# One FFN pass per batch with weights loaded by expert, fp16 loads, and k/v pooling on TensorE

## Chip, cores and metric

The kernel runs on one core of a Trainium2 chip. The metric is device time in microseconds; three runs of the kernel before gave 723.87, 724.64 and 724.81 us (median 724.64).

## What is computed

Attention with pooled keys and values, then a mixture of experts that sends each token to one of eight FFNs. q, k and v are 8 batches x 8 heads x 576 tokens x 64; tokens number 4608, the model dimension is 512, the hidden one 1024.

```python
def _attn_ref(q, k, v):
    k_p = k.reshape(B, H, Sp, 8, D).mean(axis=3)
    v_p = v.reshape(B, H, Sp, 8, D).mean(axis=3)
    scores = scale * np.matmul(q, k_p.transpose(0, 1, 3, 2))
    attn = softmax(scores)
    return np.matmul(attn, v_p)

def _moe_ref(x, expert_emb, tau, w1, w2):
    xn, en = x / norm(x), expert_emb / norm(expert_emb)
    logits = xn @ en.T / tau
    expert_idx = np.argmax(logits, axis=1)
    gate_w = softmax(logits)[np.arange(N), expert_idx]
    for e in range(E):
        mask = expert_idx == e
        h = np.maximum(x[mask] @ w1[e], 0.0)
        out[mask] = gate_w[mask, None] * (h @ w2[e])
```

The norm, the softmax and the calls that join the two parts are shortened here. All inputs and the output are fp32 in HBM. On the inputs that the reference draws, all 576 tokens of a batch choose the same expert (7, 5, 5, 1, 7, 4, 3, 4 for the eight batches); a chunk of 128 tokens that lies across two batches can hold two.

## The kernel before

Five compute engines work from their own queues: PE (TensorE, with its weight loads shown as PEld), DVE (VectorE), ACT (ScalarE), POOL (GpSimd) and SP, which here only issues DMAs. A scheduler orders the work of each engine.

*Weights.* `w1_sb` and `w2_sb` hold all eight experts in bf16. POOL issues 16 DMAs (lines 78 and 82) that read fp32 and write bf16; from the ninth on each waits until the eighth before it has landed.

*Attention*, a static loop over 8 batches and 8 heads. SP loads `q_in`, `k_in` and `v_in` of one head as 72 partitions x 512 fp32 (lines 195 to 197), with two buffers each. DVE sums eight keys and eight values (lines 201, 205). PE transposes the pooled keys twice and the pooled values once (210 to 214) and q in four fp32 pieces (220), and DVE copies q to bf16 (226). Per head two matmuls of 288 columns make the scores (238, on the two halves of the rows), and ACT the exponential (247). For every piece of at most 128 tokens PE makes eight matmuls of 73 columns (255): 64 outputs, the sum, and eight products with the expert embedding. DVE divides (262, 264), ACT squares (269), and four transposes (286) put x into `xt_all`.

*Routing* (lines 296 to 416) runs once on all 36 chunks: the expert that is most frequent in each chunk, and a list of up to twelve further (chunk, expert) pairs.

*FFN* (`ffn`, lines 112 to 142). 36 chunks of 128 tokens with their first expert, then always 12 spare passes, for pairs of the list or for nothing. A pass has 8 matmuls of 512 columns into `h_ps` (120), a relu with the gate as scale on ACT (127), 8 transposes (132), a DVE copy (135), and 8 matmuls of 512 columns into `y_ps` (137). The expert is a register value, so the address of the weights in each of the 16 matmuls is worked out at run time. A spare pass reads the output rows back, adds and stores them (lines 457 to 459).

Of the kernel before, what the change touches and what calls it, by code (L numbers as in the profile page):

```python
# [22 lines left out]
@with_exitstack
def kernel(
# [28 lines left out]
    const_pool = ctx.enter_context(tc.tile_pool(name="const", bufs=1))  # L53
    wpool = ctx.enter_context(tc.tile_pool(name="wpool", bufs=1))
    route_sb = ctx.enter_context(tc.tile_pool(name="route_sb", bufs=1))

    ident_bf = const_pool.tile([128, 128], BF16)
    make_identity(nc, ident_bf)
    ident_f16 = const_pool.tile([128, 128], FP16)
    make_identity(nc, ident_f16)  # L60
    ident_f32 = const_pool.tile([128, 128], FP32)
    make_identity(nc, ident_f32)
    tri_cand = const_pool.tile([NCAND, NCAND], BF16)
    make_upper_triangular(nc, tri_cand, val=1.0, diag=False)
    ones_col = const_pool.tile([128, 1], BF16)
    nc.vector.memset(ones_col, 1.0)
    iota8 = const_pool.tile([128, 8], FP32)
    nc.gpsimd.iota(iota8, pattern=[[1, 8]], base=0, channel_multiplier=0,
                   allow_small_or_imprecise_dtypes=True)
    cgrid = const_pool.tile([1, NCAND], FP32)  # L70
    nc.gpsimd.iota(cgrid, pattern=[[1, NCHUNK], [0, MAXE - 1]], base=0,
                   channel_multiplier=0, allow_small_or_imprecise_dtypes=True)
    enT_sb = const_pool.tile([64, H, E], FP16)

    w1_sb = wpool.tile([128, E, 4, F], BF16)
    w2_sb = wpool.tile([128, E, 8, DM], BF16)
# [12 lines left out]
    ssq_all = route_sb.tile([128, NCHUNK], FP32)

    gateoh_all = route_sb.tile([128, NCHUNK, E + 1], BF16)
    rank_e_f = route_sb.tile([1, NCHUNK, MAXE], FP32)
    rank_v_f = route_sb.tile([1, NCHUNK, MAXE], FP32)
    rank_e0_i = route_sb.tile([1, NCHUNK], I32)
    extras_i = route_sb.tile([1, NEXTRA, 3], I32)

    def seg_list(b):
        segs = []
        t0 = b * S
        t = t0  # L100
        while t < t0 + S:
            c = t // 128
            seg_end = min((c + 1) * 128, t0 + S)
            segs.append((t - t0, seg_end - t, c, t - c * 128))
            t = seg_end
        return segs

    with tc.tile_pool(name="ps_m1", bufs=2, space=bass.MemoryType.PSUM) as ps_m1:

        def m1():  # L110
            return ps_m1.tile([128, 512], FP32, name="m1")

        moe_pools = {}

        def ffn(xt_tile, gm, e_val):
            h_ps = moe_pools['h'].tile([128, F], FP32, name="h_ps")
            y_ps = moe_pools['y'].tile([128, DM], FP32, name="y_ps")
            for w in range(4):
                for fb in range(2):
                    nc.tensor.matmul(  # L120
                        out=h_ps[:, ts(fb, 512)],
                        lhsT=xt_tile[:, w, :],
                        rhs=w1_sb[:, ds(e_val, 1), w, ts(fb, 512)].squeeze(1),
                        start=(w == 0), stop=(w == 3),
                    )
            h_sb = moe_pools['sb'].tile([128, F], BF16, name="h_sb")
            nc.scalar.activation(out=h_sb, in_=h_ps, func=AF.Relu, scale=gm)  # L127
            ht_ps0 = m1()
            ht_ps = ht_ps0.bitcast(BF16)[:, 0:1024].rearrange("p (w t) -> p w t", t=128)
            h_sb8 = h_sb.rearrange("p (d w) -> p w d", w=8)  # L130
            for w in range(8):
                nc.tensor.transpose(out=ht_ps[:, w, :], in_=h_sb8[:, w, :],  # L132
                                    identity=ident_bf)
            ht_sb = moe_pools['sb'].tile([128, 8, 128], BF16, name="ht_sb")
            nc.vector.tensor_copy(out=ht_sb, in_=ht_ps)  # L135
            for w in range(8):
                nc.tensor.matmul(  # L137
                    out=y_ps,
                    lhsT=ht_sb[:, w, :],
                    rhs=w2_sb[:, ds(e_val, 1), w, :].squeeze(1),  # L140
                    start=(w == 0), stop=(w == 7),
                )
            return y_ps

        with tc.tile_pool(name="init_sb", bufs=1) as init_sb:
            emb_sb = init_sb.tile([E, DM], FP32)
            nc.sync.dma_start(out=emb_sb, in_=moe_expert_emb)
            emb_sq = init_sb.tile([E, DM], FP32)
            emb_ssq = init_sb.tile([E, 1], FP32)
            nc.scalar.activation(out=emb_sq, in_=emb_sb, func=AF.Square,  # L150
                                 accum_out=emb_ssq)
            emb_nrm = init_sb.tile([E, 1], FP32)
            nc.scalar.activation(out=emb_nrm, in_=emb_ssq, func=AF.Sqrt)
            nc.vector.tensor_scalar_add(out=emb_nrm, in0=emb_nrm, scalar1=1e-6)
            emb_rcp = init_sb.tile([E, 1], FP32)
            nc.vector.reciprocal(out=emb_rcp, in_=emb_nrm)
            nc.scalar.mul(out=emb_rcp, in_=emb_rcp, mul=1.0 / tau)
            enp_sb = init_sb.tile([E, DM], FP32)
            nc.vector.tensor_scalar_mul(out=enp_sb, in0=emb_sb, scalar1=emb_rcp)
            ent_ps = m1()  # L160
            ent_v = ent_ps[0:64, 0:H * E].rearrange("p (h e) -> p h e", e=E)
            for h in range(H):
                nc.tensor.transpose(out=ent_v[:, h, :], in_=enp_sb[:, ts(h, 64)],
                                    identity=ident_f32[:E, :E])
            nc.scalar.copy(out=enT_sb, in_=ent_v)

# [328 lines left out]
```

## Time and profile before

| | |
|---|---|
| median of three runs | 724.64 us |
| span of the profiled execution | 722.3 us (its own time is not given apart from the runs) |
| PE / PEld busy | 451.4 us (62%) / 206.7 us (29%) |
| DVE busy | 305.5 us (42%) |
| ACT busy | 157.5 us (22%) |
| POOL busy | 11.2 us (2%) |
| moved by DMA | 61.41 MB |

Busy shares are averages over stages that differ, so the stages have to be looked at one by one. A matmul's busy time is modelled and pipelined with its neighbours; the distance between the starts of two instructions says more. "issue" means that an engine waited for nothing that the profile shows: its own instruction stream held it.

### The profile page before, as it was taken

How to read it: one execution, taken by the hardware profiler on the slowest of the kernel's cores; microseconds unless marked ns; L12 is line 12 of the kernel's file. 1: busy time of each engine (PE TensorE's matmuls, PEld its weight loads, DVE VectorE, ACT ScalarE, POOL GpSimd, SP SyncE). 2: the span in 40 equal slices, each digit the busy share in tenths (PEclk: the TensorE clock that was granted, in tenths of full speed). 3: DMA queues.
4: the chain of work that ended last, by engine and by line, in shares of the span. 5: the costliest groups of instructions: out<-in, count | busy, mean ns of one | idle time of the engine just before them, and what ended most of it. 6: DMA issues, size and time to landing. Idle time of an engine off the chain costs nothing.

```text
span 722.3 us, 8926 instructions
## 1 busy us (share of the span) xinstructions
PE 451.4 (62%) x2261; PEld 206.7 (29%) x2284; DVE 305.5 (42%) x668; ACT 157.5 (22%) x263; POOL 11.2 (2%) x30
## 2 busy tenths in 40 slices
PE   0010035646465565655388888888888888888774
PEld 0000023434344343443132323222222222223221
DVE  0112169788778777843844522212212212122221
ACT  2000023343333334344311111111111111111110
POOL 4000000000000000000000000000000000000000
PEclk9999999999999999999999999999999999999996
DMA  7999954325243423400000101010011001111112
GB/s 160 229 230 229 209 160 123 113 93 156 74 131 93 128 94 106 131 21 30 0 30 30 45 30 44 30 45 30 30 45 44 30 30 45 44 59 60 59 73 88
DMA packets 27130, 61.41 MB, mean 85 GB/s; under 512 B 3528, under 2 KB 3528, under 8 KB 25040
## 3 DMA queue, kind: packets, MB, share of 16 engines
q1 hardware_dynamic: 24784, 44.07, 18.8%
q0 software_dynamic: 2304, 16.78, 11.2%
q8 instruction: 27, 0.44, 0.3%
q14 instruction: 15, 0.12, 0.1%
HBM read 65.03 MB, written 12.58 MB: 107 GB/s over the span
## 4 chain that ended last, share of the span: by engine, by line
PE 47%; DVE 23%; DMA 15%; issue 10%; ACT 4%; DVEq 0%; ACTq 0%; another core or an unknown queue 0%; SPq 0%
PE y_ps L137 18%; PE h_ps L120 17%; DMA k_in<-in_k_dram 12%; DVE vpx_all L205 6%; DVE kp_sb L201 5%; DVE x_sb L264 4%; PE m L220 3%; PE m L132 3%; PE xps L255 3%; DVE qT_sb L226 2%; ACT xps L269 2%; PE s_ps L238 2%; ACT at_tok L247 1%; DVE rsum L262 1%; DMA o_sb<-out_dram 1%
## 5 line engine op out<-in xcount | busy, mean ns | idle before, releaser
L137 PE MATMUL y_ps<-w_sb,ht_sb 128*128 x372 | 141.0, 387 | 31.8 <-issue 7.7
L120 PE MATMUL h_ps<-w_sb,xt_all 128*128 x278 | 102.1, 384 | 29.7 <-PE h_ps L120 8.0
L127 ACT ACTIVATE h_sb<-h_ps,gm 128x1024 bf16<-128x1024 f32 x48 | 53.5, 1114 | 290.0 <-PE h_ps L120 274.2
L437 DVE COPY y_sb<-y_ps 128x512 f32<-128x512 f32 x36 | 24.9, 692 | 129.6 <-PE y_ps L137 129.6
L137 PEld LDWEIGHTS <-ht_sb 128*128 128x128 bf16 x384 | 36.9, 97 | 134.3 <-issue 119.0
L201 DVE TENSOR_REDUCE kp_sb<-k_in 72x64 bf16<-72x512 f32 x64 | 64.7, 1010 | 19.5 <-DMA k_in<-in_k_dram 19.2
L205 DVE TENSOR_REDUCE vpx_all<-v_in 72x64 f16<-72x512 f32 x64 | 64.3, 1008 | 19.7 <-DMA v_in<-in_v_dram 19.6
L135 DVE COPY ht_sb<-m 128x1024 bf16<-128x1024 bf16 x48 | 32.9, 686 | 86.2 <-PE m L132 73.7
L220 PE MATMUL m<-ident_f,q_in 72*128 72x72 f32 x256 | 45.6, 338 | 27.9 <-DMA q_in<-in_q_dram 27.9
L247 ACT ACTIVATE at_tok<-s_ps 72x576 f16<-72x576 f32 x64 | 41.4, 647 | 76.0 <-PE s_ps L238 76.0
L226 DVE CAST qT_sb<-m 128x288 bf16<-128x288 f32 x64 | 29.1, 455 | 65.0 <-PE m L220 64.8
L120 PEld LDWEIGHTS <-xt_all 128*128 128x128 bf16 x288 | 27.0, 97 | 82.9 <-issue 79.3
L255 PE MATMUL xps<-vpx_all,at_tok 72*128 72x73 f16 (+1 forms) x320 | 36.8, 253 | 14.2 <-DVE dtmp L273 11.1
L286 PE MATMUL m<-ident_bf,x_sb 128*128 128x128 bf16 (+1 forms) x160 | 22.8, 293 | 36.4 <-DVE x_sb L264 36.4
L214 PE MATMUL kvt_ps<-ident_f,vpx_all 72*64 72x72 f16 x64 | 17.2, 269 | 45.2 <-DVE vpx_all L205 44.7
L238 PE MATMUL s_ps<-qT_sb,kpT_sb 64*72 64x288 bf16 x128 | 29.1, 428 | 23.8 <-ACT at_tok L247 16.0
L220 PEld LDWEIGHTS m<-ident_f,q_in 72*128 72x128 f32 x256 | 33.9, 219 | 33.7 <-issue 29.7
L120 PE MATMUL h_ps<-w_sb,xt_in 128*128 x95 | 34.5, 377 | 8.6 <-PE h_ps L120 5.1
L269 ACT ACTIVATE xps<-x_sb 128x512 f32<-128x512 bf16 (+1 forms) x40 | 24.0, 601 | 63.0 <-DVE x_sb L264 62.9
L210 PE MATMUL kvt_ps<-ident_bf,kp_sb 72*64 72x72 bf16 x64 | 16.3, 255 | 34.1 <-DVE kp_sb L201 32.5
L132 PEld LDWEIGHTS <-h_sb 128*128 128x128 bf16 x384 | 31.5, 146 | 20.7 <-issue 15.6
L255 PEld LDWEIGHTS <-at_tok 72*128 72x128 f16 (+1 forms) x320 | 26.6, 134 | 28.1 <-issue 20.5
(101 smaller groups left out, 294.8 us busy)
## 6 DMA issues: line engine op xcount, KB each, us to landing
w_sb<-in_moe_w_dram POOLq DMA_DIRECT2D x16, 1024.0 KB, 43.6
q_in<-in_q_dram SPq DMA_DIRECT2D x64, 144.0 KB
k_in<-in_k_dram SPq DMA_DIRECT2D x64, 144.0 KB
v_in<-in_v_dram SPq DMA_DIRECT2D x64, 144.0 KB
out_dram<-y_sb SPq DMA_DIRECT2D x36, 256.0 KB
o_sb<-out_dram SPq DMA_DIRECT2D x12, 256.0 KB
out_dram<-o_sb SPq DMA_DIRECT2D x12, 256.0 KB
emb_sb<-in_moe_expert_emb_dram SPq DMA_DIRECT2D x1, 16.0 KB
```

Of the source, the lines that this page charges most:

```text
L120: nc.tensor.matmul(out=h_ps[:, ts(fb, 512)], lhsT=xt_tile[:, w, :], rhs=w1_sb[:, ds(e_val, 1), w, ts(fb, 512)].squeeze(1), start=(w == 0), ...
L127: nc.scalar.activation(out=h_sb, in_=h_ps, func=AF.Relu, scale=gm)
L132: nc.tensor.transpose(out=ht_ps[:, w, :], in_=h_sb8[:, w, :], identity=ident_bf)
L137: nc.tensor.matmul(out=y_ps, lhsT=ht_sb[:, w, :], rhs=w2_sb[:, ds(e_val, 1), w, :].squeeze(1), start=(w == 0), stop=(w == 7),)
L201: nc.vector.tensor_reduce(out=kp_sb, in_=k_in.rearrange("g (j d) -> g d j", j=POOL), axis=AX.X, op=ALU.add)
L205: nc.vector.tensor_reduce(out=vpx_all[:, h, 0:64], in_=v_in.rearrange("g (j d) -> g d j", j=POOL), axis=AX.X, op=ALU.add)
L220: nc.tensor.transpose(out=qt_m[:, ts(sblk, G)].bitcast(FP32)[:, 0:G], in_=q_in[:, ts(sblk, 128)], identity=ident_f32[:G, :G])
L226: nc.vector.tensor_copy(out=qT_sb, in_=qt_m[:, 0:4 * G])
L238: nc.tensor.matmul(out=s_ps[:, j, 0:STP], lhsT=kpT_sb[ts(j, 64), h], rhs=qT_sbs[h][ts(j, 64)], start=True, stop=True,)
L247: nc.scalar.activation(out=at_tok, in_=s_tok, func=AF.Exp, scale=escale)
L255: nc.tensor.matmul(out=xps[psl, h, 0:73], lhsT=at_tok_tiles[h][:, loc0:loc0 + L], rhs=vpx_all[:, h, :], start=True, stop=True,)
L269: nc.scalar.activation(out=xps[psl, :, 0:64], in_=x_sb[psl], func=AF.Square, accum_out=ssq_all[psl, cidx:cidx + 1])
```

## The change

Nearly the whole body is new.

- All loads go through POOL's queue and write fp16. q, k and v of a batch come in three DMAs (`load_qkv`): partitions are 2 heads x 64 groups of 9 tokens, with 4 head pairs beside each other. `load_w` loads one expert's `w1` and `w2` by a register value, into one of three fixed buffers; PE addresses only fixed buffers.
- Pooling of k and v is 18 matmuls of 512 columns per batch with a 0/1 matrix `pmat`, which POOL builds with four selects after the loads of batches 0 and 1.
- q is transposed as fp16. The products with the expert embedding become 20 matmuls per batch on the transposed x, in `_route`.
- Routing is per batch (`_route`, `_expert`): the most frequent expert of 576 tokens. The square roots are a power on POOL.
- The FFN runs once per batch on 576 tokens (`ffn_steps`): `w1` is the stationary operand and x the moving one, so the hidden layer comes out transposed and needs no transposes. The relu is shared by ACT and DVE, the gate is applied to the output.
- The order is written by hand: attention of batches 0 and 1, then for each batch b its FFN steps merged with the attention steps of b + 2 by given costs (`merge`); the last two FFNs run alone.
- Any (batch, expert) pair that is left is done in a loop at the end, whose trip count is 64 if there is one such pair and 0 otherwise.

```diff
-    w1_sb = wpool.tile([128, E, 4, F], BF16)
-    w2_sb = wpool.tile([128, E, 8, DM], BF16)
-    ...
-                    nc.tensor.matmul(
-                        out=h_ps[:, ts(fb, 512)],
-                        lhsT=xt_tile[:, w, :],
-                        rhs=w1_sb[:, ds(e_val, 1), w, ts(fb, 512)].squeeze(1),
-                        start=(w == 0), stop=(w == 3),
-                    )
+    def load_qkv(b):
+        kv = inp.tile([128, 2, HP, T * D], FP16, name="kv")
+        qq = inp.tile([128, HP, T * D], FP16, name="qq")
+        ...
+        nc.gpsimd.dma_start(out=kv[:, 0], in_=view(k))
+        nc.gpsimd.dma_start(out=kv[:, 1], in_=view(v))
+        nc.gpsimd.dma_start(out=qq, in_=view(q))
+        return kv, qq
+    def load_w(e_val):
+        w1 = wpool.tile([128, 4, F], FP16, name="w1")
+        w2 = wpool.tile([128, 4, 2, DM], FP16, name="w2")
+        nc.gpsimd.dma_start(
+            out=w1,
+            in_=moe_w1[ds(e_val, 1)].squeeze(0).rearrange("(w p) f -> p w f", p=128))
+        ...
+        return w1, w2
+        def _pool():
+            ...
+            for t in range(T):
+                for par in range(2):
+                    rows = ts(par, 64)
+                    nc.tensor.matmul(
+                        out=pk[0:G, ts(par, 512)],
+                        lhsT=pmat[rows, t, :],
+                        rhs=kv[rows, :, :, ts(t, D)].rearrange("p a h d -> p (a h) d"),
+                        start=(t == 0), stop=(t == T - 1))
+        def pv(c):
+            ...
+            px = psa()
+            for h in range(H):
+                nc.tensor.matmul(
+                    out=px[0:L, h * 128:h * 128 + D + 1],
+                    lhsT=st['at', h][:, c * 128:c * 128 + L],
+                    rhs=st['vpx'][:, h // 2, h % 2, :],
+                    start=True, stop=True)
+            ...
+        def _expert():
+            ...
+            e_val = nc.values_load(ei[0:1, 0:1], engines=[ENG.Pool], min_val=0,
+                                   max_val=E - 1)
+            weights[b] = load_w(e_val)
+            nc.gpsimd.tensor_tensor(out=st['ssq'], in0=st['ssq'], in1=half_c, op=ALU.pow)
+            ...
+        def _next():
+            if b + 2 < B:
+                loads[b + 2] = load_qkv(b + 2)
+        def hgrp(w, half):
+            ...
+            ph = psf()
+            for kk in range(4):
+                nc.tensor.matmul(out=ph[:, 0:HALF], lhsT=w1v[:, kk, w // 2, w % 2, :],
+                                 rhs=xt()[:, kk, ts(half, HALF)],
+                                 start=(kk == 0), stop=(kk == 3))
+            ...
+        def yblk(c, part):
+            ...
+            for w in range(4 * part, 4 * part + 4):
+                nc.tensor.matmul(out=py[0:L, :],
+                                 lhsT=st['hT'][:, w // 2, w % 2, c * 128:c * 128 + L],
+                                 rhs=w2[:, w // 2, w % 2, :],
+                                 start=(w == 0), stop=(w == 7))
+            ...
+    with tc.manual_schedule():
+        run(attn_steps(0))
+        run(attn_steps(1))
+        for b in range(B):
+            fs = ffn_steps(lambda b=b: xt_all[:, b], lambda b=b: weights[b],
+                           lambda b=b: gates[b], store(b))
+            merge(fs, attn_steps(b + 2) if b + 2 < B else [])
+    ...
+    with tc.For_i(0, n_val, 1) as i:
+        f_val = nc.values_load(ext_i[0:1, ds(i, 1)], min_val=0, max_val=1)
+        with tc.If(f_val > 0):
+            ...
+            run(ffn_steps(lambda: xt_c, lambda: wx, lambda: gmx, finish))
```

PSUM: `psa()` gives one of two buffers of two banks, used by all attention steps; `psf()` one of four buffers of one bank, used by the FFN.

PE before, at the seam of the two layers of one FFN pass (`xt_all` is the transposed x, `ht_sb` the transposed hidden layer):

```order
L120 LDWEIGHTS xt_all
L120 ISA x3
L120 MATMUL h_ps<-w_sb,xt_all 128x512
L137 LDWEIGHTS ht_sb
L137 ISA x3
L137 MATMUL y_ps<-w_sb,ht_sb 128x512
```

PE after, at the same seam in the FFN of batch 0 and, between, the last two score steps of batch 2's attention (`pf` is a buffer of `psf()`, `pa` one of `psa()`, `at` the exponentials):

```order
L406 LDWEIGHTS w_414
L406 MATMUL pf<-xt_all,w_414 128x288
L241 LDWEIGHTS kpT
L241 MATMUL pa<-qT,kpT 72x256 [waits Activation_49]
...
L423 LDWEIGHTS hT
L423 MATMUL pf<-w_415,hT 128x512
...
L241 LDWEIGHTS kpT
L241 MATMUL pa<-qT,kpT 72x256 [waits Activation_49]
L241 LDWEIGHTS kpT
L241 MATMUL pa<-qT,kpT 72x320
L265 LDWEIGHTS at
L265 MATMUL pa<-vpx,at 128x65 [waits Activation_49]
```

The three register instructions ahead of each FFN matmul are gone, attention steps stand among the FFN's, and the first x matmul (line 265) follows the last score without FFN work between.

POOL before, the weight loads after the constants; a load that waits for a DMA semaphore waits for the eighth load before it:

```order
L71 IOTA cgrid 1x108
masks.py:199 AFFINE_SELECT ident_f_74<-ident_f_74 128x128 [waits Pool_49]
masks.py:66 AFFINE_SELECT tri_cand<-tri_cand 108x108 [waits Pool_49]
L78 DMA w_sb<-in_moe_w_dram 128x4096
L82 DMA w_sb<-in_moe_w_dram 128x4096
```

POOL after, from the loads of batch 1 to the first expert's weights:

```order
L83 DMA qq_107<-in_q_dram 128x4x576
L111 AFFINE_SELECT pmat_111<-pmat_111 64x648 [waits DVE_49]
L120 IOTA iota8_119 128x8 [waits Pool_49]
...
L141 TENSOR_TENSOR emb_n_135<-emb_n_135,half_c_125 8x1 [waits DVE_49,Activation_49]
L351 TENSOR_LOAD ei_402 [waits DVE_49]
L351 ISA x2
L89 ISA
L89 DMA w1_414<-in_moe_w1_dram 128x4x1024
L92 ISA
L92 DMA w2_415<-in_moe_w2_dram 128x4x1024
L355 TENSOR_TENSOR ssq_255<-ssq_255,half_c_125 128x5 [waits Activation_49]
L81 DMA kv_437<-in_k_dram 128x4x576 [waits DMASW0_49]
```

The weight loads move behind the expert's index, which DVE writes, and the loads of batch 2 behind them and behind a power.

## Rows read from the trace of the kernel before

**Rows 1.** The page: span, and the 40 slices of PE, DVE and granted clock.

```profile
span 722.3 us, 8926 instructions
PE   0010035646465565655388888888888888888774
DVE  0112169788778777843844522212212212122221
PEclk9999999999999999999999999999999999999996
```

**Rows 2.** Stages: length, busy us (count) by engine, clock, DMA share, GB/s.

```profile
14.70:100.00 85.30, 9.71 (x55) 6.17 (x55) 19.21 (x24) 0.00 (x0) 3.71 (x7) 1.00 0.98 221
100.00:347.00 247.00, 144.33 (x1065) 99.27 (x1065) 182.19 (x342) 96.21 (x201) 0.00 (x0) 1.00 0.32 99
347.00:357.00 10.00, 0.40 (x1) 0.18 (x2) 9.13 (x30) 3.46 (x5) 0.00 (x0) 1.00 0.00 0
357.00:626.00 269.00, 224.68 (x862) 76.46 (x880) 74.17 (x227) 41.68 (x40) 0.00 (x0) 1.00 0.10 35
626.00:722.30 96.30, 71.69 (x274) 24.16 (x277) 19.77 (x41) 12.26 (x11) 0.00 (x0) 0.94 0.20 69
```

**Rows 3.** The chain that ended last, shares of the span by line.

```profile
by line: PE y_ps L137 18.0%; PE h_ps L120 16.8%; DMA k_in<-in_k_dram 12.1%; issue 9.9%; DVE vpx_all L205 5.7%; DVE kp_sb L201 5.1%; DVE x_sb L264 3.7%; PE m L220 3.5%; PE m L132 3.1%; PE xps L255 2.8%; DVE qT_sb L226 2.3%; ACT xps L269 2.1%
```

**Rows 4.** Timeline in the FFN: start us, length us, engine, line, operation [idle before].

```profile
566.56 0.65 PE L132 MATMUL m<-ident_bf,h_sb 128*128 128x128 bf16 x8
...
569.46 0.10 PEld L137 LDWEIGHTS <-ht_sb 128*128 128x128 bf16 x1 [0.32 <-issue]
569.88 0.10 PEld L137 LDWEIGHTS <-ht_sb 128*128 128x128 bf16 x1 [0.32 <-issue]
```

**Rows 5.** Waits over the span: us in total, times, longest.

```profile
PEld L137 <- issue: 119.0, 336, 2.5
```

**Rows 6.** Groups by line: count, busy us, mean ns of one, idle before.

```profile
L247 ACT ACTIVATE at_tok<-s_ps 72x576 f16<-72x576 f32 x64 | 41.4, 647 | 76.0 <-PE s_ps L238 76.0
L201 DVE TENSOR_REDUCE kp_sb<-k_in 72x64 bf16<-72x512 f32 x64 | 64.7, 1010 | 19.5 <-DMA k_in<-in_k_dram 19.2
L226 DVE CAST qT_sb<-m 128x288 bf16<-128x288 f32 x64 | 29.1, 455 | 65.0 <-PE m L220 64.8
L135 DVE COPY ht_sb<-m 128x1024 bf16<-128x1024 bf16 x48 | 32.9, 686 | 86.2 <-PE m L132 73.7 <-PE y_ps L137 12.4
L238 PE MATMUL s_ps<-qT_sb,kpT_sb 64*72 64x288 bf16 x128 | 29.1, 428 | 23.8 <-ACT at_tok L247 16.0 <-DVE qT_sb L226 6.8 <-ACT kpT_sb L228 0.7
L264 DVE TENSOR_TENSOR x_sb<-xps,rsum 128x512 bf16<-128x512 f32 (+1 forms) x40 | 27.5, 687 | 1.0
L437 DVE COPY y_sb<-y_ps 128x512 f32<-128x512 f32 x36 | 24.9, 692 | 129.6 <-PE y_ps L137 129.6
L262 DVE RECIPROCAL rsum<-xps 128x8 f32<-128x8 f32 (+1 forms) x40 | 8.2, 206 | 17.7 <-PE xps L255 17.4
```

**Rows 7.** Timeline in attention, PE and ACT.

```profile
152.71 0.65 PE L255 MATMUL xps<-vpx_all,at_tok 72*128 72x73 f16 x8 [0.19 <-DVE dtmp L273]
...
163.60 0.46 PE L238 MATMUL s_ps<-qT_sb,kpT_sb 64*72 64x288 bf16 x2 [0.34 <-DVE qT_sb L226]
```

**Rows 8.** DMA queues: packets, MB, share of 16 engines' span (q1 SP, q0 POOL).

```profile
q1 hardware_dynamic: 24784, 44.07, 18.8%
q0 software_dynamic: 2304, 16.78, 11.2%
```

**Rows 9.** Timeline of POOL at the start.

```profile
1.13 0.29 POOL masks.py:199 TENSOR_SCALAR_AFFINE_SELECT ident_bf<-ident_bf 128x128 bf16<-128x128 bf16 x1
...
3.76 0.54 POOL L82 DMA_DIRECT2D w_sb<-in_moe_w_dram  x1
```

**Rows 10.** The chain's last pieces in time: start us, length us, what.

```profile
713.64 2.02 DMA out_dram<-o_sb
715.67 2.60 DMA o_sb<-out_dram
```

More of the change, by code (lines that the diff above doesn't have):

```diff
@@ new lines, in load_w @@
+    def load_w(e_val):
[4 more added lines that the diff above has]
+            in_=moe_w1[ds(e_val, 1)].squeeze(0).rearrange("(w p) f -> p w f", p=128))
+        nc.gpsimd.dma_start(
+            out=w2,
+            in_=moe_w2[ds(e_val, 1)].squeeze(0).rearrange(
+                "(w p r) d -> p w r d", p=128, r=2))
+        return w1, w2
+    loads = {0: load_qkv(0)}
+    ident_h = const.tile([128, 128], FP16)
@@ new lines @@
+    make_identity(nc, ident_h)
+    ident_f = const.tile([128, 128], FP32)
+    make_identity(nc, ident_f)
+    loads[1] = load_qkv(1)
+    pmat = const.tile([128, T, G], FP16)
+    nc.vector.memset(pmat, 1.0)
+    for half in range(2):
+        sl = pmat[ts(half, 64)]
+        nc.gpsimd.affine_select(out=sl, in_=sl, pattern=[[1, T], [-POOL, G]],
+                                compare_op=ALU.is_ge, fill=0.0, base=0,
+                                channel_multiplier=T)
+        nc.gpsimd.affine_select(out=sl, in_=sl, pattern=[[-1, T], [POOL, G]],
+                                compare_op=ALU.is_ge, fill=0.0, base=POOL - 1,
+                                channel_multiplier=-T)
@@ new lines @@
+    nc.scalar.activation(out=emb_sq, in_=emb, func=AF.Square, accum_out=emb_n)
+    nc.gpsimd.tensor_tensor(out=emb_n, in0=emb_n, in1=half_c[:E, 0:1], op=ALU.pow)
+    nc.vector.tensor_scalar(out=emb_n, in0=emb_n, scalar1=1e-6, scalar2=tau,
+                            op0=ALU.add, op1=ALU.mult)
+    nc.vector.reciprocal(out=emb_n, in_=emb_n)
+    nc.vector.tensor_scalar_mul(out=emb, in0=emb, scalar1=emb_n)
+    ent_ps = psa()
+    for w in range(4):
+        nc.tensor.transpose(out=ent_ps[:, ts(w, E)], in_=emb[:, ts(w, 128)],
+                            identity=ident_f[:E, :E])
@@ new lines, in out_rows, with store, finish, run @@
+    def out_rows(o_b, c, j):
+        t = TORD[2 * c + j]
+        return o_b.rearrange("(p t) d -> t p d", t=T)[t]
+    def store(b):
+        o_b = out[ts(b, S)]
+        def finish(c, L, y_sb):
+            for j in range(L // 64):
+                nc.sync.dma_start(out=out_rows(o_b, c, j), in_=y_sb[ts(j, 64)])
+        return finish
+    def run(steps):
+        for _, f in steps:
+            f()
+    def merge(a, bs):
+        ta = sum(c for c, _ in a) or 1.0
+        tb = sum(c for c, _ in bs) or 1.0
+        i = j = 0
+        ca = cb = 0.0
+        while i < len(a) or j < len(bs):
+            if j >= len(bs) or (i < len(a) and ca / ta <= cb / tb):
+                c, f = a[i]
+                i += 1
+                ca += c
+            else:
+                c, f = bs[j]
+                j += 1
+                cb += c
+            f()
@@ new lines @@
+    with tc.manual_schedule():
[5 more added lines that the diff above has]
+            merge(fs, attn_steps(b + 2) if b + 2 < B else [])
+    ext_i = keep.tile([1, B * E], I32)
+    nc.vector.tensor_scalar(out=ext_i, in0=ext_f.rearrange("p b e -> p (b e)"),
+                            scalar1=0.25, scalar2=None, op0=ALU.add)
```

681 lines of the change are left out of this document (302 added, 379 removed).

## The prediction

> **What bounds the kernel now.** I read the table of stages first [rows 2]. Attention takes the first 347 us, routing 10 us, the 36 main FFN passes 269 us and the 12 spare passes 96 us. In the first 100 us DMA is full (share 0.98) and PE does almost nothing; from 100 to 347 us DVE is busy 182 of 247 us; from 357 us on PE is busy 225 of 269 us. So three different limits follow each other, with little overlap between stages: the slices [rows 1] show PE and DVE trading places at a third of the span. The chain of the work that ended last [rows 3] agrees: 18% and 17% are FFN matmuls, 12% is waiting for a k tile, 10% is "issue".
>
> That "issue" is the point in the FFN. Two weight loads of the y matmul start 0.42 us apart, each after 0.32 us of issue; the eight transposes just before them, with nothing between load and matmul, take 0.65 us together [rows 4]. The clock is at its 2.4 GHz level in both (granted 1.00 in that stage [rows 2], full in all slices but the last [rows 1]). The order shows three register instructions ahead of each FFN matmul, because its weights are addressed by a register, and 119 us of waiting for issue stand before the y weight loads alone [rows 5]. 48 passes x 16 matmuls x 0.42 = 323 of the 365 us of the two FFN stages: these are bound by PE's instruction stream, not by its columns.
>
> **The change, part by part.** It removes 48 passes of 128 tokens and puts 8 passes of 576 tokens in their place. Counts below are from the code and the order.
>
> *FFN pass.* Per batch 64 matmuls of 288 columns and 40 of 512, each with a weight load and no register instructions. Price: the eight transposes have seven gaps in 0.65 - 0.225 us, 0.061 us for 128 columns [rows 4]; by that rate 512 columns are 0.244 and 288 are 0.137 us, together 18.5 us; at 2.4 columns per ns they would be 8.5 + 7.7 = 16.2 us. I take 17 us, with these two as ends.
>
> *Attention on PE*, per batch: the k/v pooling is 18 matmuls of 512 columns in nine pairs on the two halves of the rows. The two score matmuls of such a pair start 0.03 us apart (0.46 us for both, 0.428 for one [rows 6, 7]), so pairs overlap: 9 x 0.244 = 2.2 us; if the pooling pairs don't, 4.4. Then 20 q transposes, 8 k transposes, 40 small x matmuls, 20 x transposes and 21 routing matmuls at 0.061 (eight x matmuls take 0.65 us today [rows 7], the same spacing), 6.6 us, and 8 score pairs at 0.15, 1.2 us. Sum 10.0; upper end 13 with the dearer pooling and slower weight loads. I take 10.6.
>
> *What DVE loses.* 128 reductions of 1.01 us [rows 6] (5.7% and 5.1% of the chain [rows 3]) go away, replaced by the pooling matmuls. Per batch DVE keeps 8 relus (288 columns, 0.455), 3 y copies (0.692), 5 reciprocals and products (0.206 + 0.687), 2 q copies (1152/1024 x 0.686), one k, one v and five x copies (about 0.5 each, 3.5) and some 25 small routing operations priced like a reciprocal: 20 us. ACT has 8 exponentials (0.647), 8 relus, 5 squares priced like an exponential, 2 y copies and two k copies: 15 us [rows 6]. Both stay under PE's 28.
>
> *Transfers.* All input loads move to Pool's queue with a cast to fp16. Today's weight loads move 33.5 MB of fp32 in 11.2% of 722.3 us of all engines, 81 us or 415 GB/s; the SP queue moved 44.07 MB in 136 us, 324 GB/s [rows 8]. Per batch: weights 4.2 MB, 10.1 us; q, k, v 3.5 MB, 8.5 us; output 1.2 MB, 3.6 us; 22 us under a period of 33, and each load is issued a period ahead. The runs are shorter (2.3 and 4 KB read instead of 16), which I price at nothing while the slack of 11 us holds; the 2 KB packets of SP's queue moved at 324 GB/s, which would make it 27.
>
> *The start.* Pool's row is six loads, two identities, four selects of 64 x 648, iotas, and only then a power that the embedding needs; PE's first matmul waits for that and everything else queues behind it. An issue is 0.54 us for 128 runs and a select 0.29 for 128 columns [rows 9]. With 512 runs and 648 columns: 0.54 to 2.2, and 0.29 to 1.5. I take 1.0 for both (neither is likely to scale fully): 0.5 + 6 + 1 + 4 + 1.5 for iotas and the power + 1.5 for the embedding = 14.5 us; ends 9 and 24. Batch 0's loads land by 12 us, covered.
>
> *Attention of batches 0 and 1* runs alone, each step waiting for the one before. Pooling 3; copies of k, v and q on DVE in a row until the first score 3.4; eight exponentials through two PSUM buffers 5.9; five x chunks, each 0.65 + 0.206 + 0.687 + a copy of 0.45 on DVE, partly overlapped, 8.1; routing until PE can go on 2.4: 22.8 us, twice 45.6. PE enters the FFN at 60 us. Batch 0's weights are chosen at 39 us and landed by 52; the loads of batch 2 are queued behind them and land at 60, just in time.
>
> *Six merged periods* (FFN of b with attention of b+2). PE work 17 + 10.6. Stalls: in the score stretch ACT has seven exponentials and two or three relus, 5.6 us, against PE's 3.7, so 1.9; the first x matmul stands right behind the eighth score and waits for its exponential, 0.9; four x chunks wait for DVE's 0.9 + 0.2 with some 0.7 of FFN between, 1.6; the first y matmul and routing 1.0. Period 33 us, six 198 us.
>
> *Two passes alone*, 17 + 0.9 each: 36 us. *The end*: the last copy 0.7, store 0.34 + 2.0 [rows 10], and registers, a branch and barriers on five engines round a loop of zero trips, for which no row stands: between 0 and 10, I take 4, since a store's whole wait is 2. 7 us.
>
> Sum: 60 + 198 + 36 + 7 = 301 us of span. The runs are 723.87 to 724.81 (median 724.64) where the span is 722.3, so 2.3 lie around it: **303 us**.
>
> The Trainium skill has a rule that speaks against this: "SBUF — State Buffer", section "SBUF: two separate sides", says that Pool and DVE share a pair of SBUF ports as an exclusive lock, and that a Pool DMA's descriptors can't be written while DVE runs an operation that takes both. No row of before shows an issue slowed by it.
>
> **Rivals.**
> *Loads set the period.* Five issues per batch on Pool are 2.7 to 11 us by the bounds above. If Pool could write them only while DVE stood idle (13 of 33 us), or if the shorter runs halved the transfer rate (37 + 4 us), PE would wait for each batch's data: period 40, 303 + 6 x 7 = 345, with both late start and tail 345 to 420. For it: everything is now on one in-order queue, and Pool also waits there for the expert index. Against: a period of lead and 11 us of slack. (The skill's rule above is one way to this.)
> *Register instructions were not the cause.* If a 512-column matmul costs 0.42 us anyway and a 288-column one 0.24, a pass is 32 us, a period 48: 60 + 288 + 66 + 7 + 2 = 423. Against: 0.32 of every 0.42 is issue [rows 4, 5].
> *Better cover than I allow.* Stalls of 1 us instead of 5.4 and a start of 9: 303 - 26 - 6 - 6 = 265.
> *Slower than before: the loop at the end runs.* One flagged (batch, expert) pair makes it 64 trips, each with barriers, and each flagged pair adds a pass with its own weight load: 10 + 17 + five round trips of 2.6 + 2.0 through one buffer [rows 10], 50 us. To lose, 421 us must come together: eight pairs, or 6.6 us per empty trip. The reference run on its inputs shows one expert for all 576 tokens of every batch, with the second choice at least 0.034 lower in logits of up to 1.3; fp16 changes of 0.05% don't reach that. So the loop should have no trip.
>
> **How the numbers follow.** Forecast case (270 to 345) 0.74; better cover, below 270, 0.10; loads 0.11; matmul rate 0.03; loop 0.02. The range: start -5/+9, the two attentions -6/+10, the periods -24 (29 us) to +36 (39 us), tail and end -5/+8; not all at one end, so 270 to 350, which leaves out about 0.17. This kernel can be told from no change within about 0.2%; faster 0.975, same 0.005, slower 0.02.
>
> **What would show it.** Right: FFN weight loads 0.12 to 0.25 us apart with little issue before them; PE over 80% busy from 60 us on; six stretches of about 33 us; no trip of the last loop; Pool's issues finished before 14 us. Wrong: PE waiting for a DMA of kv or of the weights, Pool's issues of over 2 us, pooling pairs 0.24 us apart, PE's granted clock at the lower level in the single attentions, or long waits of the x matmuls for DVE.

## The result, and the profile after

The changed kernel takes **313.47 us** (median of 4 runs, 312.87 to 315.35) against 724.47 for the kernel before on the same chip: a ratio of 0.433, interval 0.4317 to 0.4343. The forecast was 303, its range 270 to 350. Its profiled execution, the slowest of the four (315.35 us), has a span of 313.8 us. One of e10's four runs below, 315.19 us, was in a slower state of the chip and is left out of its time and ratio.

The page of the changed kernel: busy time, three of the rows with 40 slices, and POOL's DMA queue (packets, MB, share of 16 engines).

```profile
span 313.8 us, 5182 instructions
...
PE 245.4 (78%) x1980; PEld 141.0 (45%) x1981; DVE 144.7 (46%) x445; ACT 108.2 (34%) x252; POOL 45.1 (14%) x65
...
PE   0376737689995999869995989599995999299990
...
DVE  1135552745563637363664455363835456332410
...
PEclk9985565589998699979999899969997999789998
...
q0 software_dynamic: 21120, 30.94, 56.3%
...
HBM read 61.88 MB, written 9.44 MB: 227 GB/s over the span
```

Against [rows 1] the three stages have become one: PE is busy in nearly every slice from the eighth on. Two things stand out. PE's row has regular holes (a 5 among 9s, and a 2 near the end), and the granted clock dips to 5 or 6 at the start and to 6 to 8 behind most holes. The dip at the start is hardly new. The trace of before has no record of the clock ahead of 361.9 us, and the page shows the full clock where there is none. In its attention four transposes of 128 columns took 0.61 us:

```profile
151.91 0.61 PE L286 MATMUL m<-ident_bf,x_sb 128*128 128x128 bf16 x4
```

In its FFN eight took 0.65 at the full clock [rows 4]. In the changed kernel four take 0.61 where the granted clock is 0.50 (at 28.74) and 0.39 where it is 1.00 (at 83.40). By this pace PE went at about the lower level in the attention of before, too, though no clock record shows it.

The stages of the changed kernel, columns as in [rows 2]: the start, the two single attentions, the six merged periods, the rest.

```profile
0.00:13.10 13.10, 0.42 (x4) 0.47 (x5) 1.91 (x10) 2.02 (x4) 9.95 (x23) 1.00 0.89 145
13.10:35.40 22.30, 16.03 (x145) 8.98 (x144) 9.41 (x24) 9.18 (x20) 0.00 (x0) 0.69 0.43 75
35.40:61.50 26.10, 16.21 (x143) 9.32 (x143) 12.26 (x43) 9.30 (x21) 5.02 (x6) 0.57 0.85 149
61.50:264.60 203.10, 176.57 (x1483) 100.95 (x1483) 105.53 (x323) 78.35 (x186) 27.37 (x33) 0.93 0.75 140
264.60:313.80 49.20, 36.14 (x210) 21.28 (x209) 15.61 (x45) 9.33 (x21) 2.77 (x3) 0.91 0.47 97
```

A merged period is 203.1 / 6 = 33.85 us (forecast 33), and PE is busy 87% of it. The matmuls themselves, in the timeline of PE: pooling at the start and in a merged period, then the second half of one FFN pass and both halves of the next.

```profile
13.17 4.05 PE L179 MATMUL pa<-kv,pmat 64*72 64x512 f16 x18
...
93.76 2.13 PE L179 MATMUL pa<-kv,pmat 64*72 64x512 f16 x18
...
280.73 8.91 PE L423 MATMUL pf<-w,hT 128*128 128x512 f16 x40
289.58 8.02 PE L406 MATMUL pf<-xt_all,w 128*128 128x288 f16 x64
297.43 8.91 PE L423 MATMUL pf<-w,hT 128*128 128x512 f16 x40
```

By the distances of these starts a pass is 7.85 + 8.85 = 16.7 us: matmuls of 512 columns start 0.22 us apart where before they stood 0.42 apart [rows 4]. Eighteen pooling matmuls take 2.13 us, 0.24 a pair, so the two row halves do overlap; the same eighteen at 13 us take 4.05. The trace has no record of the clock there (the first is at 18.1 us); at 62.64 us, where the granted clock is 0.50, eighteen took 3.71.

**The hole in each period.** The timeline of all engines across the end of attention 2. In brackets: idle time before, and what ended it.

```profile
95.17 0.14 DVE L349 TENSOR_SCALAR ei<-ei_f 1x1 int32<-1x1 f32 x1
95.82 1.65 PE L406 MATMUL pf<-xt_all,w 128*128 128x288 f16 x12
...
97.09 0.74 POOL L89 DMA_DIRECT2D w<-in_moe_w_dram  x1 [27.68 <-issue]
97.83 0.76 POOL L92 DMA_DIRECT2D w<-in_moe_w_dram  x1
98.58 1.21 POOL L355 TENSOR_TENSOR ssq<-ssq,half_c 128x5 f32<-128x5 f32 x1
...
99.83 0.17 DVE L357 TENSOR_SCALAR rn<-ssq 128x5 f32<-128x5 f32 x1 [4.52 <-POOL ssq L355]
...
100.57 0.24 ACT L367 ACTIVATE lg<-lg 128x40 f32<-128x40 f32 x1 [8.87 <-DVE lg L364]
100.71 0.39 ACT L411 ACTIVATE hT<-pf 128x288 f16<-128x288 f32 x1
...
101.15 3.12 PE L406 MATMUL pf<-xt_all,w 128*128 128x288 f16 x12 [3.68 <-ACT hT L411]
```

Read it from the bottom. PE's h matmuls stand 3.68 us for a relu, `hT`, because all four FFN accumulators (`psf()`) are full. That relu is next on ACT behind the routing's exponential (L367), which waits for DVE. DVE stands 4.52 us in its own queue, with its half of the relus behind it, for the power L355. POOL can't do that power sooner, since it comes third behind the two weight loads, and these need the expert index that DVE wrote at 95.17 and that reaches POOL's first issue at 97.09. The power needs none of that: its operand, the sums of squares, was ready before the routing began. It is only written behind the loads. The waits of the whole span say how often (us in total, times, longest):

```profile
ACT lg L367 <- DVE lg L364: 68.0, 8, 9.2
...
DVE rn L357 <- POOL ssq L355: 34.7, 8, 4.9
...
PE pf L406 <- ACT hT L411: 25.7, 11, 5.6
```

and of the six merged periods, for PE alone, every wait of 0.8 us or more in total:

```profile
PE pf L406 <- ACT hT L411: 20.1, 10, 4.0
PE pa L265 <- ACT at L248: 2.4, 6, 0.4
PE pa L265 <- DVE x_sb L274: 2.4, 7, 0.4
PE pa L241 <- ACT at L248: 1.0, 6, 0.2
PE pa L330 <- DVE oh_all L322: 0.8, 1, 0.8
```

No DMA is among them. The clock falls with each of these holes: from 100.0 to 106.8 us the granted clock is 0.50, the 1.2 GHz level, then 1.00 until 137.6, just behind the next hole.

### The profile page after: what moved, and what is told of

Its sections match the earlier page's. It is cut to its first block, busy times and chain, and to the rows that moved or that the text cites. A ratio compares the mean times of both kernels' runs of the same rounds, so it can differ in the third digit from the quotient of the medians.

```text
span 313.8 us, 5182 instructions
## 1 busy us (share of the span) xinstructions
PE 245.4 (78%) x1980; PEld 141.0 (45%) x1981; DVE 144.7 (46%) x445; ACT 108.2 (34%) x252; POOL 45.1 (14%) x65
## 3 DMA queue, kind: packets, MB, share of 16 engines
q0 software_dynamic: 21120, 30.94, 56.3%
HBM read 61.88 MB, written 9.44 MB: 227 GB/s over the span
## 4 chain that ended last, share of the span: by engine, by line
PE 60%; DVE 14%; ACT 9%; POOL 8%; issue 5%; POOLq 1%; DVEq 0%; ACTq 0%
PE pf L423 20%; PE pf L406 19%; ACT at L248 6%; DVE x_sb L274 4%; PE pa L265 4%; PE pa L241 4%; PE pa L206 3%; PE pa L179 3%; POOL ssq L355 3%; DVE y_sb L434 2%; PE pa L312 2%; POOL w L92 2%; PE pa L285 2%; DVE kpT L224 1%; ACT hT L411 1%
## 5 line engine op out<-in xcount | busy, mean ns | idle before, releaser
L406 PE MATMUL pf<-xt_all,w 128*128 128x288 f16 x512 | 84.5, 313 | 25.7 <-ACT hT L411 25.7
L423 PE MATMUL pf<-w,hT 128*128 128x512 f16 (+1 forms) x320 | 78.7, 380 | 0.0
L406 PEld LDWEIGHTS <-w 128*128 128x128 f16 x512 | 50.4, 106 | 48.6 <-issue 31.1
L248 ACT ACTIVATE at<-pa 72x576 f16<-72x576 f32 x64 | 38.4, 646 | 16.7 <-PE pa L241 16.6
L413 DVE TENSOR_SCALAR hT<-pf 128x288 f16<-128x288 f32 x64 | 27.9, 450 | 29.2 <-PE pf L406 29.0
L423 PEld LDWEIGHTS <-hT 128*128 128x128 f16 (+1 forms) x320 | 28.3, 100 | 25.8 <-issue 0.8
L411 ACT ACTIVATE hT<-pf 128x288 f16<-128x288 f32 x64 | 25.6, 408 | 41.0 <-PE pf L406 41.0
L296 ACT ACTIVATE sq<-x_sb 128x512 f16<-128x512 f16 (+1 forms) x40 | 24.9, 625 | 20.0 <-DVE x_sb L274 19.8
L274 DVE TENSOR_TENSOR x_sb<-pa,r 128x512 f16<-128x512 f32 (+1 forms) x40 | 27.6, 690 | 2.8 <-ACT sq L296 0.5
L367 ACT ACTIVATE lg<-lg 128x40 f32<-128x40 f32 x8 | 1.9, 236 | 68.0 <-DVE lg L364 68.0
L272 DVE RECIPROCAL r<-pa 128x8 f32<-128x8 f32 (+1 forms) x40 | 8.1, 203 | 30.7 <-PE pa L265 30.7
L179 PE MATMUL pa<-kv,pmat 64*72 64x512 f16 x144 | 22.1, 462 | 0.0
L285 PE MATMUL pa<-ident_h,x_sb 128*128 128x128 f16 (+1 forms) x160 | 16.7, 234 | 2.3 <-DVE x_sb L274 2.3
L207 DVE COPY qT<-pa 128x1152 f16<-128x1152 f16 x16 | 12.1, 756 | 12.7 <-PE pa L206 12.5
```

Of the source, the lines that this page charges most:

```text
L179: nc.tensor.matmul(out=pk[0:G, ts(par, 512)], lhsT=pmat[rows, t, :], rhs=kv[rows, :, :, ts(t, D)].rearrange("p a h d -> p (a h) d"), start ...
L248: nc.scalar.activation(out=at, in_=pS[0:G, c0:c0 + S], func=AF.Exp, scale=escale)
L274: nc.vector.tensor_tensor(out=x_sb[0:L], in0=pxv[:, :, 0:D], in1=r[0:L].unsqueeze(2).to_broadcast([L, H, D]), op=ALU.mult)
L296: nc.scalar.activation(out=sq[0:L], in_=xf[0:L], func=AF.Square, accum_out=st['ssq'][0:L, c:c + 1])
L406: nc.tensor.matmul(out=ph[:, 0:HALF], lhsT=w1v[:, kk, w // 2, w % 2, :], rhs=xt()[:, kk, ts(half, HALF)], start=(kk == 0), stop=(kk == 3))
L411: nc.scalar.activation(out=dst, in_=ph[:, 0:HALF], func=AF.Relu)
```

## The experiments

**e1: the power alone is moved**, from behind the weight loads to the first line of the step before.

```
 def _route():
+    nc.gpsimd.tensor_tensor(out=st['ssq'], in0=st['ssq'], in1=half_c, op=ALU.pow)
...
     weights[b] = load_w(e_val)
-    nc.gpsimd.tensor_tensor(out=st['ssq'], in0=st['ssq'], in1=half_c, op=ALU.pow)
```

> Edit: the power on POOL (line 355) is issued at the start of the routing step, ahead of the load of the expert's index and of the two weight loads, instead of behind them. Theory A: at the end of each period DVE waits 4.5 us for this power, which stands in POOL's queue behind the index and two issues of 0.75 us; ACT's next relu stands behind the exponential that waits for DVE, so PE stops for 3.7 to 5.6 us and then runs at half clock for 3.4 to 6.8 us. Then 31 us of PE waits and up to 15 us of half clock go: 270 to 283 us. Rival B: something else in the same chain is late next (the weights, or DVE's own gate operations), and less than 10 us go: above 303 us.

Measured: **275.18 us** (274.49 to 275.42), ratio 0.3793 [0.3787, 0.380]. The six merged periods in its table of stages, between the same two matmuls (line 330 before, 331 here) as in the changed kernel:

```profile
57.70:231.30 173.60, 165.80 (x1483) 96.03 (x1484) 104.95 (x323) 79.03 (x186) 27.59 (x34) 0.99 0.86 167
```

and its timeline, POOL in one period and PE at the last routing:

```profile
86.38 1.19 POOL L309 TENSOR_TENSOR ssq<-ssq,half_c 128x5 f32<-128x5 f32 x1 [21.94 <-ACT sq L296]
...
91.63 0.80 POOL L89 DMA_DIRECT2D w<-in_moe_w_dram  x1 [4.07 <-DVE ohe L373]
...
234.66 6.21 PE L406 MATMUL pf<-xt_all,w 128*128 128x288 f16 x48 [1.24 <-ACT hT L411]
```

One moved instruction is worth 38 us. The same matmuls in the six periods take 173.6 us instead of 203.1: PE's idle time falls from 26.5 to 7.8 us, and the matmuls themselves take 165.8 us instead of 176.6, since the clock stays up (0.99 against 0.93). So the holes cost twice: 18.7 us of waiting, and 10.8 us of matmuls at the lower clock behind them. Of the 40.4 us between the two profiled spans 29.5 lie there, 3.8 in the second single attention (26.1 to 22.3) and 7.1 in the last stage (49.2 to 42.1). The last routing's hole shrinks from 5.61 to 1.24 us.

**e10: more work on PE.** If holes and the clock behind them cost that much, then pooling each merged batch twice (18 more matmuls; the second round overwrites the first with the same sums) should cost less than its length.

```
-for t in range(T):
+for t in (list(range(T)) * 2 if b > 1 else range(T)):
```

> Edit: the changed kernel with the pooling matmuls of batches 2 to 7 made twice over into the same PSUM buffer (the second pass overwrites the first with the same sums), 18 more matmuls per period, which in all but the first and last period stand just before the stop of PE. Theory (the clock counts): PE's stop of 3.7 us shrinks to 1.6 and PE stays at full clock behind it; the added 6 x 2.1 us are mostly hidden in the stop, and most of the half-clock stretches (31 us behind the stops, worth up to 15) go: 300 to 308 us in spite of more work. Rival (the clock falls anyway, or costs little): 313 to 318 us.

Measured: 308.36 us (308.25 to 309.01), ratio 0.4256 [0.4247, 0.4266], below the changed kernel's 0.433 and just above the range that was expected. Its merged stage, and PE's largest wait:

```profile
61.50:259.00 197.50, 180.78 (x1589) 103.57 (x1590) 105.17 (x324) 78.23 (x186) 27.36 (x33) 0.97 0.77 144
```

```profile
PE pf L406 <- ACT hT L411: 15.7, 11, 5.6
```

With 108 matmuls more the kernel is faster. The added pairs run inside the hole, so the wait for the relu falls from 25.7 to 15.7 us, and only three stretches at half clock follow the holes, 10.2 us together, where there were six with 30.7. PE's busy time in the merged stage rises by 4.2 us (176.6 to 180.8), though 6 x 2.13 = 12.8 us of pooling were added. This shows the hole's second price without touching POOL.

**e2: the start.** The forecast said that PE's first matmul waits for everything ahead of the power on POOL. Batch 1's three loads are moved behind the selects.

```
-loads[1] = load_qkv(1)        # ahead of pmat's selects
...
+loads[1] = load_qkv(1)        # behind them
```

> Edit: the three loads of batch 1 are issued after the four selects that build the pooling matrix instead of before them. Theory: the first matmul (12.7 us) waits for POOL's queue alone, so it comes 2.3 us (three issues of 0.77) earlier and the time falls by the same to 311 us. Rival: the loads of batch 0 are late next, or batch 1's come too late; no change, 313.5 us, or slower.

Measured: 313.34 us (312.50 to 314.01), ratio 0.4322 [0.4313, 0.4331]: not to be told from the changed kernel. Timelines of POOL and PE at the start, the changed kernel first, then e2:

```profile
7.01 1.68 POOL L111 TENSOR_SCALAR_AFFINE_SELECT pmat<-pmat 64x648 f16<-64x648 f16 x2
...
11.02 0.58 POOL L141 TENSOR_TENSOR emb_n<-emb_n,half_c 8x1 f32<-8x1 f32 x1
...
12.68 0.56 PE L148 MATMUL pa<-ident_f,emb 8*128 8x8 f32 x4 [12.68 <-DVE emb L145]
```

```profile
10.95 0.58 POOL L141 TENSOR_TENSOR emb_n<-emb_n,half_c 8x1 f32<-8x1 f32 x1
...
12.61 0.56 PE L148 MATMUL pa<-ident_f,emb 8*128 8x8 f32 x4 [12.61 <-DVE emb L145]
```

The embedding's power is the last of POOL's operations either way, so the order of those ahead of it changes nothing. My expectation took the three loads as out of PE's way once they stood behind the selects, though they still stood ahead of the power; that was wrong.

**e3 and e7: both single attentions merged.** e3 interleaves attentions 0 and 1 (with more buffers for `qT` and `x_sb`, fewer for the squares and `y_sb`), e7 also issues batch 2's loads at the start.

```
-run(attn_steps(0))
-run(attn_steps(1))
+merge(attn_steps(0), attn_steps(1))
```

> Edit: the attention steps of batches 0 and 1 are merged with each other step by step instead of one batch after the other (some buffer counts are changed to make room: q copies 4, x 4, squares 1, y 3). Theory: the 48 us from 13 to 61 us are bound by latencies between engines, not by any engine (PE 32 us modelled at half clock, DVE 22, ACT 18), so two batches side by side need some 33 to 38 us: 298 to 304 us. Rival: the two PSUM buffers of the attention steps hold the steps one behind the other anyway, and less than 5 us go: above 308 us.

Measured for e3: 335.54 us (334.22 to 336.55), ratio 0.4627 [0.4614, 0.4639], slower by 22 us. Both attentions end at 53 us instead of 61.5, and then, in the timelines:

```profile
52.81 0.22 PE L330 MATMUL pa<-oh_all,ones_m 128*128 128x40 f16 x1 [0.36 <-DVE oh_all L322]
...
58.42 0.17 DVE L357 TENSOR_SCALAR rn<-ssq 128x5 f32<-128x5 f32 x1 [4.34 <-POOL ssq L355]
...
61.99 0.14 DVE L349 TENSOR_SCALAR ei<-ei_f 1x1 int32<-1x1 f32 x1
63.40 1.14 PE L406 MATMUL pf<-xt_all,w 128*128 128x288 f16 x4 [10.37 <-DMA w<-in_moe_w_dram]
...
84.11 4.06 PE L179 MATMUL pa<-kv,pmat 64*72 64x512 f16 x18 [19.57 <-DMA kv<-in_v_dram]
```

PE first waits for batch 0's weights, with nothing left to run beside their transfer. The second expert's index comes only at 61.99 us, since DVE stands for the first one's power again (58.42). Its weights are issued at 63.40, and behind them, on one queue, stand the loads of batches 2 and 3, so PE waits a second time.

> Edit: as e3 (attention of batches 0 and 1 merged with each other), with the three loads of batch 2 issued in the beginning, behind batch 1's, instead of behind the weight loads. Theory: e3 lost because its late choice of the experts put all of the next loads on POOL's queue at once, and PE waited 19.6 us for the values of batch 2; with these loads early that wait goes, and only the wait for the first weights stays: 314 to 319 us against e3's 335.5. Rival: the merged attentions themselves or their smaller buffers are what is slow, and e3's time stays: 330 to 336 us.

Measured for e7: 314.06 us (313.02 to 314.96), ratio 0.4331 [0.4317, 0.4345]. With batch 2 loaded early the second wait is gone and the first stays (10.47 us, PE waiting for the weights at 63.48). What the merge gains, the wait for the first weights takes.

**e9: the same idea one batch later**, with e8 (below): attention 0 alone, 1 and 2 merged, then FFN b with attention b + 3.

```
-run(attn_steps(1))
+merge(attn_steps(1), attn_steps(2))
...
-    merge(fs, attn_steps(b + 2) if b + 2 < B else [])
+    merge(fs, attn_steps(b + 3) if b + 3 < B else [])
```

> Edit: as e8, with attention of batch 0 alone, then batches 1 and 2 merged with each other while the first weights load, then each FFN b merged with attention b + 3, and three FFNs alone at the end (gate buffers 5, q copies 4, x 4, squares 1, y 3). Theory: two attentions side by side take some 30 us, and one merged period of 29 us becomes an FFN alone of 17: 267 us. Rival: the two attentions side by side take the 37 us or more that the two of e3 took: 274 us or above.

Measured: 283.40 us (282.66 to 283.77), ratio 0.3909 [0.390, 0.3918], 10 us slower than e8. One stretch of its table of stages, and one line of PE's timeline in it:

```profile
70.00:107.00 37.00, 30.89 (x276) 17.58 (x275) 24.62 (x99) 13.92 (x34) 9.85 (x14) 0.92 0.97 186
```

```profile
106.74 4.06 PE L180 MATMUL pa<-kv,pmat 64*72 64x512 f16 x18 [4.04 <-DMA kv<-in_v_dram]
```

Weights and inputs of two batches are issued together from 74 to 88 us; DMA is full (0.97) and PE waits. The period with this wait, FFN 1's, takes 35.0 us (102.0 to 137.0) where e8's takes 28.9: some 6 of the 10 us. The other 4 are the rival of the expectation: the two attentions side by side took 37.7 us (33.6 to 71.3), 15.8 more than e8's second one alone (21.9), and an FFN alone in place of a merged period gives back only 12. This was a miss of mine: in e9 as behind 63 us in e3, two batches in step ask for their transfers in step.

**e4: without the loop at the end.** Everything from `ext_i` on is removed.

> Edit: the loop at the end and the values that steer it are left out; for these inputs it has no trip, so the output is whole. Theory of the prediction: registers, branch and barriers round a loop without trips cost 4 us: 309.5 us. Rival: they lie under the last store, which lands some 2.4 us after its issue: 312 to 313.5 us.

Measured: 310.44 us (309.34 to 312.02), ratio 0.4285 [0.4273, 0.4298]: 3 us less, 1.4 to 5.1 by the two intervals. No matmul follows 306.4 us in the changed kernel, so the loop makes no trip.

**e5 and e6: the kernel before, with one part of the change.** e5 has each main pass's expert as a constant of the program (the spare passes take expert 0), so PE has no register instructions; e6 leaves the 12 spare passes out.

```
-rhs=w1_sb[:, ds(e_val, 1), w, ts(fb, 512)].squeeze(1),
+rhs=w1_sb[:, e_val, w, ts(fb, 512)],          # e5; w2_sb likewise
...
-for i in range(NEXTRA):
+for i in range(0):                             # e6
```

> The kernel before, with the expert of each FFN matmul written as a constant (the main passes take the expert of the batch in which the chunk begins, the spare passes expert 0, so the rows that a spare pass should add come out otherwise), so that no register instruction stands ahead of a matmul. Theory: these instructions are what makes 0.42 us per matmul; with 0.216 us a main pass loses 16 x 0.2 = 3.3 us, 36 of them 119 us; a spare pass is then held at 5.6 us by its output's round trip and 12 lose 29: 576 us (560 to 595). Rival: a 512-column matmul costs 0.42 us for another reason, 724 us.

Measured for e5: 583.74 us (583.40 to 584.07), ratio 0.8055 [0.8041, 0.8068]. The group of the y weight loads (columns as in [rows 6]):

```profile
L137 PEld LDWEIGHTS <-ht_sb 128*128 128x128 bf16 x384 | 36.9, 101 | 67.6 <-issue 23.7 <-DVE ht_sb L135 9.6
```

The 119.0 us of waiting for issue [rows 5] are 23.7, and 141 us of the time are gone: the register instructions were the FFN's limit.

> The kernel before without its twelve spare passes; the four chunks that hold tokens of a second expert lack them. Theory: the stage from 626 us to the end goes but for the last store, 92 us: 632 us. Rival: the end of the main passes is slower than the spare ones show, for instance since the stores pile up: above 640 us.

Measured for e6: 649.38 us (648.87 to 650.42), ratio 0.8966 [0.8951, 0.8981]: 75 us less, where I expected 92. The y copies of the main passes, from first to last, in the kernel before and in e6:

```profile
L437 DVE COPY y_sb<-y_ps x36: 691/692/693, 368.7 to 625.9; 128x512 f32<-128x512 f32 x36
```

```profile
L437 DVE COPY y_sb<-y_ps x36: 691/692/693, 390.8 to 643.5; 128x512 f32<-128x512 f32 x36
```

So the passes are about as long (252.7 us, 257.2 before) and start 22 us later: without the spare passes DVE works off the list of further pairs ahead of the main ones (its end, line 416, is at 382.7 us, before at 420.6), work that lay beside passes before. The time is in the rival's range, above 640, though not for the rival's reason. The spare passes themselves cost the 96.3 us of their stage [rows 2], of which e6 gives back 75.

**e8 and e11: a better version.** e8 is e1 with the embedding's power ahead of all loads but batch 0's, and the loads of batches 1 and 2 right behind it. e11 is e8 with the second single attention cut: what follows its scores (the x chunks and the routing) runs merged with FFN 0 instead of alone.

```
 nc.gpsimd.tensor_tensor(out=emb_n, in0=emb_n, in1=half_c[:E, 0:1], op=ALU.pow)
+loads[1] = load_qkv(1)
+loads[2] = load_qkv(2)
...
-run(attn_steps(1))
+rest = attn_steps(1); run(rest[:12]); rest = rest[12:]      # e11
...
+    merge(fs, rest + attn_steps(b + 2) if b + 2 < B else [])
+    rest = []
```

> Edit: as e1, and in the beginning POOL does the selects, the iotas and the embedding's power before it issues the loads of batches 1 and 2 (batch 2's come from behind the first weights). Theory: e2 changed nothing since the first matmul waits for the embedding's power, the last of POOL's operations there; with the power ahead of the loads PE begins 2.3 us earlier: 272 to 273.5 us against e1's 275.2. Rival: the loads of batch 0 are late next: 275 us.

Measured for e8: 273.46 us (271.95 to 274.19), ratio 0.3773 [0.3755, 0.379]; PE's first matmul waits 10.4 us instead of 12.7. The gain over e1 is at the edge of what the intervals can tell.

> Edit: as e8, with the attention of batch 1 cut after its scores: the first part runs alone while the first weights land, and its second part is merged, ahead of batch 2's attention, with the FFN of batch 0 (gate buffers 4). Theory: the second part of an attention alone takes some 11 us, bound by DVE's latencies; beside FFN work it costs PE about 5, and the FFN of batch 0 starts when its weights land, near 46 us: 267 to 270 us against e8's 273.5. Rival: batch 1's expert is then chosen so late that its weights and batch 3's loads make PE wait, as in e3: 273 us or above.

Measured for e11: **268.73 us** (267.76 to 269.44), ratio 0.3702 [0.3693, 0.371], the fastest of all. Its stages from the first FFN on:

```profile
45.00:80.00 35.00, 31.53 (x323) 19.32 (x320) 22.52 (x68) 18.15 (x44) 4.96 (x6) 0.94 0.73 138
80.00:225.00 145.00, 138.16 (x1251) 80.19 (x1247) 88.70 (x274) 65.67 (x155) 23.82 (x28) 1.00 0.87 169
```

FFN 0 begins at 46 us instead of 61.5, and from 80 to 225 us PE is busy 95% at full clock. What is left is PE's own work, 229 us of 267.

## Why the prediction was right, point by point

The time was right, 313 for 303, and so was the mechanism of the change: one FFN pass per batch without register instructions, with attention beside it. Among its terms the stall at the routing was wrong, and another error hid most of it.

*Right.* The register instructions: 141 us by e5. The FFN pass, 16.7 us (taken 17). Pooling by overlapping pairs, 2.13 (2.2). The start, 13.2 us (14.5), though with other pieces: an issue is 0.745 to 0.917 us and a select about 0.8 (1.0 taken for both). Attention 0, 13.2 to 35.5 us, 22.3 (22.8). PE's work in a merged period, 165.8 / 6 = 27.6 us in e1 (27.6). The end, 306.4 to 313.8, 7.4 us (7), of it about 3 for the loop (4). Pool's issues are finished by 14 us, and the loop makes no trip. One sign of being wrong was ill put: "pooling pairs 0.24 us apart" is what was measured, and it is the forecast's own price of 9 x 0.244 for pairs that overlap.

*Right by two errors that cancel: the period.* The working gave 27.6 us of PE work and 5.4 of stalls: 4.4 in the score and x stretches, 1.0 for "the first y matmul and routing". Measured, the score and x stretches wait 5.8 us in six periods, 1.0 each; ACT and DVE, at 13.1 and 17.6 us per period, have more room than I gave them. The routing takes the rest: 33.85 - 27.6 - 1.0 = 5.25 us; by e1's comparison it is 3.1 of waiting and 1.8 of slower matmuls, which e1 gives back, and 0.3 more. So 4.4 + 1.0 was 1.0 + 5.25: the period came out by luck. The step that failed is the term "first y matmul and routing 1.0", with the 4.4 beside it too high. The prediction said of the start what POOL's power there stands behind and who waits for it. It did not ask the same of the other power, which stands behind two issues on POOL, with DVE and ACT in order behind it. The rival "better cover" (265 us) was in reach of that one line: e1 makes 275, and its periods are 28.9 us (that rival's: 33 - 4.4 = 28.6).

*Wrong: the second single attention and the last two passes.* Attention 1 took 26.1 us (22.8), which includes the same wait for the power (PE stands 4.51 us for DVE); in e1 it is 22.3. The last two passes took 264.6 to 306.4, 41.8 us (36): the hole of the last routing, 5.61 us, and 48 matmuls behind it in 8.54 us where the full rate (64 in 7.85) makes 5.9.

*A sign of wrong that came true: the clock.* In the single attentions the granted clock is 0.69 and 0.57, with PE busy 16 of 22 us. Attention 0 is as long as forecast all the same. A likely reason: prices such as 0.65 us for eight x matmuls [rows 7] came from the attention of before, which by its pace went at the lower level, too. What a single attention would take at the full clock no run shows. The clock's price that no term had was in the merged periods.

*Loads.* The rival "loads set the period" is not what happened: no wait of PE in the merged periods is for a DMA. The shorter runs were priced at nothing, but the loads did get slower: HBM read 61.88 MB, while q0's packets took 56.3% of 313.8 us, 177 us, so 350 GB/s where the weight loads of before moved at 415 [rows 8]. That is 19% more time, covered by the slack; no run changes the length of the runs alone, so the cause isn't shown. e3 and e9 show where the cover ends: when two batches ask together. POOL's issues in the changed kernel (count, ns min/median/max, first and last start; k loads, first weight loads):

```profile
L81 POOL DMA_DIRECT2D kv<-in_k_dram x8: 774/801/917, 1.5 to 203.0; - x8
```

```profile
L89 POOL DMA_DIRECT2D w<-in_moe_w_dram x8: 745/745/801, 38.5 to 268.2; - x8
```

None of POOL's issues is longer than 0.917 us, the very first, with DVE busy half of the time. The Trainium skill's exclusive lock between POOL and DVE ("SBUF — State Buffer", section "SBUF: two separate sides") would keep POOL from writing descriptors while DVE holds both ports. These rows show no issue stretched by it; whether any of DVE's operations here takes both ports no row shows, so the rule itself isn't tested.

*Where 411 us went.* Each alone, in the kernel before, the register instructions were worth 141 us (e5) and the spare passes 75 (e6). These don't simply add, since a quarter of the passes with register instructions are spare ones. What remains, about 195 us or somewhat more, goes to the rest of the change: fewer, larger passes, pooling on PE, and attention and FFN side by side. No run here takes that apart further.

## What to carry to other kernels

On in-order queues, look at what each engine's next instruction waits for *and what stands ahead of the one that it waits for*: a helper operation of 1.2 us, written behind two loads whose address comes late, stopped DVE and ACT in each of eight batches and PE, for 3.4 to 5.6 us, in seven, and moving one line was worth 38 us of 313. A hole in PE is paid twice where the clock falls behind it, so filling or closing it is worth more than its length. Overlapping two batches in step also puts their transfers in step, which cost e9 some 6 us; cutting off only the tail of one, as e11 does, gained 5.

## What the runs showed of the hardware that I had not expected

- Behind each of six holes of 3.4 to 5.6 us PE's granted clock was at the 1.2 GHz level for 3.4 or 6.8 us. In e10, with the holes partly filled, it fell behind those of 1.75, 2.11 and 5.59 us and not behind three of 1.42 to 1.44. Before, with the engine busy 84% in the FFN [rows 2], it stayed up from 361.9 to 703 us.
- A power on POOL takes 0.58 us for 8 x 1 elements and 1.2 us for 128 x 5.
- From DVE's write of the expert index (95.17 us, 0.14 long) to POOL's first issue that uses it (97.09) 1.8 us pass.
- Casting loads with runs of 2.3 and 4 KB read 350 GB/s in the changed kernel, those with runs of 16 KB 415 before; the runs' length was not the only difference.
